# A leaky ReLU cut into two instructions, and a new order for the head of a kernel

## The chip, the cores and the metric

The kernel runs on one core of a Trainium2 chip. The metric is the device time of one launch in microseconds (us), as the median of several runs. Work inside the core is split over engines with a queue of their own each: TensorE (PE) multiplies matrices, VectorE (DVE) and GpSimd (POOL) do elementwise work, ScalarE (ACT) does activations and copies, SyncE (SP) starts transfers. An instruction starts when it is first in its engine's queue and the semaphores that it waits for have been raised.

## The reference

```python
def _attn_ref(x):                      # x: (8, 3008, 256)
    X = np.fft.fft(x, axis=1)
    X = np.fft.fft(X, axis=2)
    return X.real.astype(np.float32)

def _moe_ref(x, w_in, w_out):          # x: (24064, 256), w_in: (256, 2048), w_out: (2048, 256)
    h = x @ w_in
    g = np.maximum(0.01 * h, h)        # leaky ReLU
    return (g @ w_out).astype(np.float32)
```

The real part of a two-dimensional Fourier transform of each of 8 batches is taken, its rows go through a projection up to 2048 columns, a leaky ReLU, and a projection down to 256.

## The kernel before

The feature transform is folded into the weights: `fold_w_in` multiplies `w_in` by the cosine and sine tables, and gives `wf`. Of the transform along the sequence, a cosine part (`mixc`) and a sine part (`mixs`) are formed, and each hidden block is the sum of the two products for one column and the difference for the mirrored column. So a sum and a difference of two PSUM banks stand ahead of each leaky ReLU.

The work is laid out as chunks of columns. Most chunks go down with a scheme of sums and products that saves matmuls (class `Chunk`, lines 1173 to 1269 of the profile's rows). The first two pieces of 251 columns, `PLAIN = 2`, go straight through, since at the start the weights are still being loaded and converted: they are the **plain steps**. There are 16 of them, one for each piece `j` and pair `f` of hidden blocks; step n has f = n // 2 and j = n % 2 up to the last two, which are swapped. A plain step has these parts:

- `R:n` (`raised`, L951): eight PE rows in the trace, four into each of two PSUM banks of the ring `cos_psa, sin_psa, cos_psb, sin_psb`.
- `A:n` (`activate`): the cosine product gets its Nyquist term, either on DVE (L964, twice) or, for the steps of `SEEDED` and what follows them, by seeds that ACT writes into the bank ahead of the matmuls (L943, twice) and a copy (L960). Then DVE forms the sum (L971) and the difference (L972), 128x502 each, and ACT applies the leaky ReLU (L974) to both.
- `D0:n` and `D1:n` (`down_plain`, L996): four matmuls each (eight rows in the trace) that add the step's share to the lower or upper half of the output columns. Piece 0 adds into `sum_psa` and `sum_psb`, piece 1 into `sum_psc` and `dft_ps`. In each half the matmuls of the sum (r = 0) come ahead of those of the difference (r = 1).

Between the steps stands the work on the weights. `L:` starts a load on SP. `C:` converts one loaded block on DVE (L633, L642, L643 finish it, L625 and L626 begin the next, ACT's L627 and L628 stand between). `S:k` forms the sum and the difference of the two halves of a block of `w_in` (L675), on the engines of `HALVES_ON`: both on DVE for k = 1, both on POOL for k = 2, one on each for k = 3. `F:k` is the fold (L690): one PE group for the sum, one for the difference, and copies on ACT (L694). `T` loads four tables, `N` and `NF` load and fold the Nyquist column (POOL), `W:` forms sums of `w_out` on POOL (L718).

The order of all this is written out by hand: the text `HEAD` lists it, each word being issued to its engines in turn, and the dictionary `START` goes on with it beside the first steps of the first ordinary chunk. An instruction keeps its place in its own engine's queue, so two words that use different engines can change places without any effect.

```python
for op in HEAD.split():
    do(op)
rest()
```

In `START` the activations of steps 12 to 15 are not issued at once but handed on (`later`), and one ACT instruction (L1445) does them.

Of the kernel before, what the change touches and what calls it, by code (L numbers as in the profile page):

```python
# [12 lines left out]
ALU = mybir.AluOpType  # L13
ACT = mybir.ActivationFunctionType

B, S, D, F = 8, 3008, 256, 2048
# [25 lines left out]
NF = F // P  # L42
# [8 lines left out]
    0: "C:o6 D0:10 R:12 A:12",  # L51
    1: "D1:10 M:o7",
    2: "R:13 A:13",
    3: "D0:11 E:o7 W:2 W:3",
    4: "R:14 A:14 D1:11",
    5: "D0:12",
    6: "R:15 A:15",
    7: "D1:12",
# [2 lines left out]
    10: "D0:14",  # L61
    12: "D1:14",
    15: "D0:15",
    17: "D1:15",
}
ORDER = "w0a w0b o0 o1 w1a w1b o2 o3 w2a w2b o4 o5 w3a w3b o6 o7"
LOADED_EARLY = "o1 w1a w1b o2"
HEAD = """
L:o3 D0:0 R:1 B:o1 D1:0 A:2 R:3 C:o1 A:1 A:3 L:w2a C:w1a D0:2 D0:1 C:w1b D1:2 L:w2b D1:1 S:1 D0:3 F:1 D1:3 C:o2 R:4 L:o4 L:o5 A:4 C:o3 R:5 A:5 D0:4 C:w2a T D1:4 R:6 A:6 L:w3a D0:5 R:7 D1:5 C:w2b A:7 L:w3b L:o6 S:2 D0:6 F:2 C:o4 N D1:6 R:8 A:8 D1:7 C:o5 R:9 A:9 D0:7 NF D0:8 R:10 D0:9 C:w3a L:o7 A:10 C:w3b R:11 S:3 A:11 D1:8 F:3 D1:9 W:1 W:0
"""  # L70
EARLY = 14
FIRST_DOWN = 18.1
# [244 lines left out]
def tile_fnet_leaky_relu(  # L317
# [15 lines left out]
    nc = tc.nc  # L333
# [26 lines left out]
    def ring(tag):  # L360
        r = rings[tag]
        r[0] += 1
        return r[1][(r[0] - 1) % len(r[1])]
# [564 lines left out]
    def hidden_blocks(j, f):  # L928

        return 2 * f, 2 * f + 1  # L930

    def up(j, f):
        raised(j, f)
        activate(j, f)
# [3 lines left out]
    def seed_plain(j, f):  # L938

        b, c, at, n, _ = blocks[j]  # L940
        pt = seeded[j, f] = [up_ps(), up_ps()]
        for h, fh in enumerate(hidden_blocks(j, f)):
            nc.scalar.activation(pt[0][:, h * n : (h + 1) * n], nb_sb[:, at : at + n], ACT.Copy, scale=wn[:, fh : fh + 1])  # L943
# [11 lines left out]
    def activate(j, f, later=None):  # L955
        b, c, at, n, _ = blocks[j]
        fs, pt = hidden_blocks(j, f), raw.pop((j, f))
        cos = ring("cos")
        if (j, f) in seeded:
            nc.scalar.copy(cos[:, 0 : 2 * n], pt[0][:, 0 : 2 * n])  # L960
        else:
            for h in range(2):
                hs = slice(h * n, (h + 1) * n)
                nc.vector.scalar_tensor_tensor(cos[:, hs], in0=nb_sb[:, at : at + n],  # L964
                                               scalar=wn[:, fs[h] : fs[h] + 1],
                                               in1=pt[0][:, hs], op0=ALU.mult, op1=ALU.add)
        step = steps.index((j, f)) + 1
        if step in SEEDED:
            seed_plain(*steps[step])
        g = ring("g")[:, 0 : 4 * n].rearrange("p (r k) -> p r k", r=2)  # L970
        nc.vector.tensor_tensor(g[:, 0], cos[:, 0 : 2 * n], pt[1][:, 0 : 2 * n], op=ALU.add)  # L971
        nc.vector.tensor_tensor(g[:, 1], cos[:, 0 : 2 * n], pt[1][:, 0 : 2 * n], op=ALU.subtract)  # L972
        if later is None:
            nc.scalar.activation(g, g, ACT.Lrelu)  # L974
        else:
            later.append([g])
        a = [[g[:, r, h * n : (h + 1) * n] for h in range(2)] for r in range(2)]
        hidden[j, f] = a
# [506 lines left out]
    def do(op, later=None):  # L1485
# [17 lines left out]
        elif kind in ("R", "A", "D0", "D1"):  # L1503
            step = steps[int(at)]
            if kind == "R":
                raised(*step)
            elif kind == "A":
                activate(*step, later=later)
            else:
                down_plain(*step, halves=(int(kind[1]),))  # L1510
        elif kind == "S":
            sums_of[at] = sums_of_w_in([loaded[f"w{at}{a}"] for a in "ab"], [getattr(nc, e) for e in HALVES_ON[int(at) - 1]])
        elif kind == "F":
            fold_w_in(int(at) * WN, WN, [loaded.get(f"w{at}{a}") for a in "ab"], sums=sums_of.get(at))
        elif kind == "T":
            even_tables[:] = [[ring("s") for _ in range(2)] for _ in range(2)]
            for part in range(2):
                for i, first in enumerate((0, DW[0][0])):
                    nc.sync.dma_start(even_tables[part][i][:, 0 : DW[0][i]], direct_even[part, :, first : first + DW[0][i]])
        elif kind == "N":  # L1520
            nc.sync.dma_start(nyx, x_nyq)
        elif kind == "NF":
            fold_nyquist(0)
            rows = Rows(nya[:, 0], [nyz], 0, 0)
            rows.fold_even(nc.gpsimd)
            rows.fold_odd(nc.gpsimd)
            nyq_of.append(rows)
        else:
            assert kind == "W", op
            sum_weights(int(at))  # L1530
# [7 lines left out]
    with tc.manual_schedule(engines={mybir.EngineType.DVE, mybir.EngineType.PE, mybir.EngineType.SP}):  # L1538
        with tc.manual_schedule(engines={mybir.EngineType.Pool, mybir.EngineType.Activation}):
# [87 lines left out]
            store_nyquist(1, nyq_t)  # L1627
            spread_rest()
            activate(*steps[0])
            o.mantissa()  # L1630
            o.end()
# [45 lines left out]
```

## Time and profile before

| | us |
|---|---|
| median of 4 runs | 1822.67 (1822.64 to 1822.72) |
| the profiled execution | 1822.71 |
| its span, first to last instruction | 1820.9 |
| PE busy | 1811.0 (99%) |
| DVE busy | 1544.8 (85%) |
| ACT busy | 1135.6 (62%) |
| POOL busy | 1085.3 (60%) |

The profile comes from one execution. A row of a timeline has its start, how long it lasts (for merged rows, all of them together), the engine, the source line, the operation with its tiles, and in brackets how long the engine had been idle and which instruction released it. A matmul in float32 is two rows in the trace. Successive matmuls overlap, so the distance between two starts, and not a row's length, is what a group costs PE.

### The profile page before, as it was taken

The page shows a single profiled execution, that of the slowest core. Times are in us where ns is not written, and L with a number is a line of the kernel's source. Part 1 is how long each engine was busy: PE and PEld are TensorE (multiplying, and loading weights), DVE is VectorE, ACT ScalarE, POOL GpSimd, SP SyncE. Part 2 cuts the span into 40 slices and gives each one's busy share as a digit, 9 for nine tenths or more (in the row PEclk, how much of TensorE's full clock was granted, in tenths as well). Part 3 has the DMA queues.
Part 4 walks back from the last instruction along what each step waited for, and adds up shares of the span by engine and source line. Part 5 has one row for each costly group of instructions (what it writes and reads, how often), then busy time and mean ns, then how long its engine had stood idle before and what let it go on. Part 6 is the DMA issues. An engine that isn't in the chain of part 4 may idle for free.

```text
span 1820.9 us, 27070 instructions
## 1 busy us (share of the span) xinstructions
PE 1811.0 (99%) x9408; PEld 1540.0 (85%) x9408; DVE 1544.8 (85%) x3216; ACT 1135.6 (62%) x2319; POOL 1085.3 (60%) x590
## 2 busy tenths in 40 slices
PE   9999999999999999999999999999999999999999
PEld 7788888888888888888888888888888888888888
DVE  8869998897888978899787988879888798787678
ACT  4768666675666756566565666657666576565551
POOL 0156666565666665666665666656666666666660
PEclk9999999999999999999999999999999999999999
DMA  7312121202102011021101112010121110010000
GB/s 249 107 48 89 30 69 35 72 14 71 31 28 72 21 65 31 29 70 35 58 24 32 67 35 73 18 68 24 32 73 35 52 30 29 24 35 13 10 18 31
DMA packets 65897, 88.61 MB, mean 49 GB/s; under 512 B 10064, under 2 KB 53456, under 8 KB 65760
## 3 DMA queue, kind: packets, MB, share of 16 engines
q1 hardware_dynamic: 65616, 86.88, 14.5%
q8 instruction: 74, 1.21, 0.3%
q14 instruction: 63, 0.52, 0.1%
q10 hardware_dynamic: 144, 0.00, 0.0%
HBM read 62.12 MB, written 24.72 MB: 48 GB/s over the span
## 4 chain that ended last, share of the span: by engine, by line
PE 94%; DVE 4%; issue 1%; ACT 1%; POOL 0%; DMA 0%; DVEq 0%; POOLq 0%; ACTq 0%
PE sum_psc L1224 21%; PE sum_psa L1224 17%; PE sum_psb L1224 17%; PE cos_psa L1173 9%; PE sin_psa L1173 9%; PE cos_psb L1173 8%; PE sin_psb L1173 8%; PE dft_ps L756 3%; PE dft_ps L996 1%; DVE block L1203 1%; PE sum_psc L996 0%; PE sum_psb L996 0%; PE sum_psa L996 0%; DVE part L1269 0%; DVE block L971 0%
## 5 line engine op out<-in xcount | busy, mean ns | idle before, releaser
L1203 POOL TENSOR_TENSOR block<-block 128x752 f32<-128x752 f32 (+2 forms) x540 | 1045.4, 1948 | 609.0 <-DVE xt L1017 176.2
L1445 ACT ACTIVATE block<-block 128x376 f32<-128x376 f32 (+5 forms) x718 | 426.5, 623 | 4.3 <-DVE block L1186 3.6
L1203 DVE TENSOR_TENSOR block<-block 128x752 f32<-128x752 f32 (+2 forms) x328 | 416.6, 1274 | 0.2
L1186 DVE TENSOR_TENSOR block<-cos,sin_psa 128x376 f32<-128x376 f32 (+2 forms) x510 | 251.0, 533 | 140.8 <-PE sin_psa L1173 136.6
L1224 PEld LDWEIGHTS sum_psc<-block,wt 128*128 128x128 f32 x1736 | 289.3, 190 | 45.8 <-issue 0.5
L1224 PE MATMUL sum_psc<-block,wt 128*128 128x188 f32 (+2 forms) x1736 | 327.3, 321 | 0.4 <-DVE part L1269 0.4
L1186 DVE TENSOR_TENSOR block<-cos,sin_psb 128x376 f32<-128x376 f32 (+2 forms) x482 | 240.1, 539 | 102.8 <-PE sin_psb L1173 101.6
L1224 PE MATMUL sum_psa<-block,wt 128*128 128x188 f32 (+2 forms) x1736 | 312.2, 321 | 0.0
L1224 PEld LDWEIGHTS sum_psa<-block,wt 128*128 128x128 f32 x1736 | 283.5, 190 | 22.8
L1179 ACT COPY cos<-cos_psa 128x376 f32<-128x376 f32 (+2 forms) x255 | 119.0, 467 | 248.3 <-PE cos_psa L1173 245.6
L1179 ACT COPY cos<-cos_psb 128x376 f32<-128x376 f32 (+2 forms) x241 | 113.6, 472 | 210.8 <-PE cos_psb L1173 210.7
L1173 PE MATMUL cos_psa<-mixc,wf 128*128 128x376 f32 (+2 forms) x510 | 199.8, 473 | 0.5 <-ACT cos_psa L1168 0.5
L1173 PE MATMUL sin_psa<-mixs,wf 128*128 128x376 f32 (+2 forms) x510 | 199.8, 473 | 0.0
L1173 PE MATMUL sin_psb<-mixs,wf 128*128 128x376 f32 (+2 forms) x482 | 191.5, 479 | 0.0
L1173 PE MATMUL cos_psb<-mixc,wf 128*128 128x376 f32 (+2 forms) x482 | 191.4, 478 | 0.0
L1269 DVE TENSOR_TENSOR part<-part 128x188 f32<-128x188 f32 (+2 forms) x462 | 187.9, 444 | 1.9
L1224 PE MATMUL sum_psb<-block,wo 128*128 128x188 f32 (+2 forms) x992 | 188.0, 321 | 0.0
L1224 PEld LDWEIGHTS sum_psb<-block,wo 128*128 128x128 f32 x992 | 165.3, 190 | 22.8
L1224 PEld LDWEIGHTS sum_psb<-block,wt 128*128 128x128 f32 x992 | 163.5, 190 | 22.8
L1224 PE MATMUL sum_psb<-block,wt 128*128 128x188 f32 (+2 forms) x992 | 177.0, 321 | 0.0
L1168 ACT ACTIVATE cos_psa<-nb,wn 128x376 f32<-128x376 f32 (+2 forms) x255 | 145.9, 572 | 8.2
L1173 PEld LDWEIGHTS sin_psa<-mixs,wf 128*128 128x128 f32 x510 | 96.6, 189 | 61.7 <-DVE block L1186 0.4
(214 smaller groups left out, 1957.5 us busy)
## 6 DMA issues: line engine op xcount, KB each, us to landing
xt<-in_x_dram SPq DMA_DIRECT2D x28, 1024.0 KB, 5.4
out_dram<-part SPq DMA_DIRECT2D x176, 94.0 KB, 1.7
out_dram<-part SPq DMA_DIRECT2D x64, 94.5 KB, 1.7
tabe<-in_seq_tab_dram SPq DMA_DIRECT2D x29, 190.0 KB, 2.6
nb<-nyq_dram SPq DMA_DIRECT2D x23, 188.0 KB, 3.9
block<-in_w_in_dram SPq DMA_DIRECT2D x8, 512.0 KB, 5.6
block<-in_w_out_dram SPq DMA_DIRECT2D x8, 512.0 KB, 4.1
xt<-in_first_x_dram SPq DMA_DIRECT2D x4, 768.0 KB, 8.3
```

Source lines behind the costliest of these rows:

```text
L756: nc.tensor.matmul(o, lhsT=still, rhs=moving, start=(i == 0), stop=(i == 3), skip_group_check=True)
L996: nc.tensor.matmul(sums[j][d][:, r * n : (r + 1) * n], lhsT=wo[:, fs[h] // 4, fs[h] % 4, d], rhs=a[r][h], start=(f == 0 and r == 0 and h = ...
L1168: nc.scalar.activation(cos_ps[self.half(f)][:, 0 : self.w], columns_of(nb_sb, self.u, self.j, self.w), ACT.Copy, scale=wn[:, f : f + 1])
L1173: nc.tensor.matmul(bank[:, 0 : self.w], lhsT=wf[:, i, f * P : (f + 1) * P], rhs=columns_of(mix_sb[i], self.u, self.j, self.w), start=(i == ...
L1179: nc.scalar.copy(copy, cos[:, 0 : self.w])
L1186: nc.vector.tensor_tensor(block.row(to, g, self.n), x, y, op=op)
L1203: ins = (engine or nc.gpsimd).tensor_tensor(self.value(16 + i), xa, ya, op=ALU.add if sign > 0 else ALU.subtract)
L1224: nc.tensor.matmul(to, lhsT=weight(w)[:, g], rhs=self.value(v)[:, g], start=(first and at == 0), stop=(last and g == 3), skip_group_check= ...
L1269: ins = nc.vector.tensor_tensor(part_of[self.copy[v]][:, 0:n], xa, ya, op=ALU.add if sign > 0 else ALU.subtract)
L1445: nc.scalar.activation(to, to, ACT.Lrelu)
```

## The change

Two things are changed. In `activate`, a plain step's leaky ReLU becomes two instructions, one after the sum and one after the difference, each 128x502, where it was one of 128x1004; for the steps of `START` it stays as it is. And the lists `HEAD` and `START` get another order: `D1:2` goes ahead of `D0:1`, `D1:5` ahead of `D0:5` and `R:7`, `D0:8` behind `R:10`, `D1:9` ahead of `D1:8` and `F:3`, `D1:11` and `D1:15` one step earlier, beside words that move past words of other engines.

```diff
@@ START
-    3: "D0:11 E:o7 W:2 W:3",
-    4: "R:14 A:14 D1:11",
+    3: "D0:11 E:o7 D1:11 W:2 W:3",
+    4: "R:14 A:14",
...
-    17: "D1:15",
+    16: "D1:15",
+    17: "",
@@ HEAD
-L:o3 D0:0 R:1 B:o1 D1:0 A:2 R:3 C:o1 A:1 A:3 L:w2a C:w1a D0:2 D0:1 C:w1b D1:2 L:w2b D1:1 S:1 D0:3 F:1 D1:3 C:o2 R:4 L:o4 L:o5 A:4 C:o3 R:5 A:5 D0:4 C:w2a T D1:4 R:6 A:6 L:w3a D0:5 R:7 D1:5 C:w2b A:7 L:w3b L:o6 S:2 D0:6 F:2 C:o4 N D1:6 R:8 A:8 D1:7 C:o5 R:9 A:9 D0:7 NF D0:8 R:10 D0:9 C:w3a L:o7 A:10 C:w3b R:11 S:3 A:11 D1:8 F:3 D1:9 W:1 W:0
+L:o3 D0:0 R:1 B:o1 D1:0 A:2 R:3 C:o1 A:1 A:3 D0:2 L:w2a C:w1a C:w1b D1:2 D0:1 L:w2b S:1 D1:1 D0:3 F:1 D1:3 R:4 C:o2 L:o4 L:o5 A:4 C:o3 R:5 A:5 D0:4 C:w2a D1:4 R:6 L:w3a A:6 D1:5 T C:w2b D0:5 R:7 D0:6 A:7 S:2 L:w3b L:o6 F:2 C:o4 D1:6 R:8 A:8 N D1:7 R:9 C:o5 D0:7 A:9 R:10 NF C:w3a D0:8 A:10 L:o7 D0:9 C:w3b R:11 S:3 D1:9 W:1 D1:8 W:0 A:11 F:3
@@ activate
-        nc.vector.tensor_tensor(g[:, 0], cos[:, 0 : 2 * n], pt[1][:, 0 : 2 * n], op=ALU.add)
-        nc.vector.tensor_tensor(g[:, 1], cos[:, 0 : 2 * n], pt[1][:, 0 : 2 * n], op=ALU.subtract)
-        if later is None:
-            nc.scalar.activation(g, g, ACT.Lrelu)
-        else:
+        for r, op in enumerate((ALU.add, ALU.subtract)):
+            nc.vector.tensor_tensor(g[:, r], cos[:, 0 : 2 * n], pt[1][:, 0 : 2 * n], op=op)
+            if later is None:
+                nc.scalar.activation(g[:, r], g[:, r], ACT.Lrelu)
+        if later is not None:
             later.append([g])
```

## The prediction

> **What bounds the kernel now.** I read the page, then the busy times by stretch, then TensorE's own timeline between 30 and 92 us, because the change touches only the head of the program and the head is the only long stretch with holes in TensorE.
>
> ```profile
> PE 1811.0 (99%) x9408; PEld 1540.0 (85%) x9408; DVE 1544.8 (85%) x3216; ACT 1135.6 (62%) x2319; POOL 1085.3 (60%) x590
> ```
>
> TensorE (PE) is busy 1811.0 of 1820.9 us. No matmul is added or removed, so the time can move only by PE's waiting: 9.9 us in all. The windows say where the head's share lies and who is full beside it.
>
> ```profile
> 20.00:40.00 20.00, 18.90 (x92) 15.92 (x91) 19.16 (x44) 8.15 (x12) 0.00 (x0) 1.00 0.64 208
> 40.00:60.00 20.00, 19.41 (x86) 15.55 (x85) 17.49 (x33) 14.57 (x22) 0.00 (x0) 1.00 0.53 181
> 60.00:80.00 20.00, 19.29 (x87) 15.98 (x86) 16.18 (x30) 14.51 (x25) 5.95 (x10) 1.00 0.20 62
> 80.00:100.00 20.00, 19.04 (x84) 15.27 (x83) 16.52 (x30) 13.34 (x25) 11.30 (x10) 1.00 0.10 27
> ```
>
> Columns: PE, weight loads, DVE, ACT, POOL, granted clock (1.00 throughout, so no clock effect is expected). DVE is busy 19.16 of 20 us in the first of these: there it sets the pace, and PE's holes are its shadow. PE's timeline names each hole (in brackets the idle time and its releaser):
>
> ```profile
> 38.93 1.97 PE L996 MATMUL sum_psc<-block,wo 128*128 128x251 f32 x8 [0.57 <-ACT block L974]
> ...
> 45.88 1.13 PE L690 MATMUL sin_psa<-part,block 128*128 128x512 f32 x2
> ...
> 51.72 1.12 PE L951 MATMUL sin_psa<-mixc,wf 128*128 128x251 f32 x4 [0.41 <-ACT sin_psa L943]
> ...
> 53.87 1.97 PE L996 MATMUL sum_psa<-block,wo 128*128 128x251 f32 x8 [0.19 <-ACT block L974]
> ...
> 61.64 1.11 PE L951 MATMUL sin_psa<-mixc,wf 128*128 128x251 f32 x4 [0.71 <-ACT sin_psa L943]
> ...
> 66.85 1.02 PE L690 MATMUL sin_psb<-part,block 128*128 128x512 f32 x2
> 67.70 1.02 PE L690 MATMUL cos_psa<-block 128*128 128x512 f32 x2
> ...
> 82.70 1.11 PE L951 MATMUL sin_psb<-mixc,wf 128*128 128x251 f32 x4 [0.33 <-ACT sin_psb L943]
> ...
> 86.77 1.12 PE L690 MATMUL sin_psa<-part,block 128*128 128x512 f32 x2 [0.41 <-DVE part L675]
> 88.11 1.12 PE L690 MATMUL cos_psb<-block 128*128 128x512 f32 x2 [0.22 <-POOL block L675]
> ```
>
> The pipelined ends hide part of each hole, so I count **start delays**: unstalled, one half-step D takes 1.70 us from start to start (40.74 to 42.44), one R 1.70 (its two rows 0.85 each), one F 0.97 + 0.85 (45.88, 46.85, 47.70). Delays: 38.93 is 0.73 late (36.50 + 1.70 = 38.20), 45.88 0.04, 51.72 0.56, 53.87 0.34, 61.64 0.87 (59.07 + 1.70), 82.70 0.49, 86.77 0.57, 88.11 0.37 (86.77 + 0.97). Sum 3.97 us: the most that this change can reach. The delay at 29.64 (DVE's conversion L643) is ahead of everything moved and stays.
>
> **What the instruction queues become.** Built and compared, DVE and POOL keep their order; ACT keeps it too, but for twelve Lrelus made two each and two output copies moved up at 139.7; SP moves one weight load ahead of four table loads. So what the new table does is reorder PE: in the head one pair of D halves is swapped and three D halves pass R or F groups; two more move later.
>
> **The split.** Rows:
>
> ```profile
> L974 ACT ACTIVATE block<-block 128x1004 f32<-128x1004 f32 x12 | 12.5, 1042 | 14.2 <-DVE block L972 14.2
> ...
> L1445 ACT ACTIVATE block<-block 128x500 f32<-128x500 f32 x16 | 9.8, 610 | 0.0
> ```
>
> Half a Lrelu takes 0.61 by the 500-wide row. Today it starts when the difference (L972) ends and lasts 1.04. After, the first half starts when the sum (L971) ends, 0.59 earlier, and the second when the difference ends, done 1.04 - 0.61 = 0.43 earlier. ACT issues the next instruction about 0.09 before an end (79.55 after 78.60 + 1.04), so a pair costs 2 x 0.52 instead of 0.95: about 0.09 us more of ACT, twelve times 1.1 us, hidden because ACT works 14.6 of 20 us here at most and the pair still ends earlier.
>
> **Walk along PE, hole by hole** (lead = how much earlier than today).
>
> ```profile
> 45.14 0.69 DVE L675 TENSOR_TENSOR part<-block 128x512 f32<-128x512 f32 x1
> ```
>
> - 38.93: D1:2 now stands ahead of D0:1, so D0:1 comes 1.70 later and its Lrelu is there. Lead 0.73.
> - 45.88 (F:1) needs DVE's sum L675, done at 45.14 + 0.69 = 45.83. DVE's queue is the same and full, so that time stays. PE arrives near 45.1 and waits. **Lead back to 0.**
> - 51.72 (R:5) waits for the seeds L943 (50.71 + 0.96); ACT's queue ahead of them follows F:1. Stays.
> - 53.87 (D0:4): first half ready at 52.8, second at 53.38; PE wants them at 53.53 and 54.4. Lead 0.34; the seeds of R:6 (56.03 + 0.99 = 57.02) cut it to 0.3.
> - 61.64 (R:7): D1:5 now fills the 0.87 in front of it. Lead 1.17.
> - 66.85 (F:2): PE arrives at 65.7, but needs the two POOL sums:
>
> ```profile
> 64.76 1.27 POOL L675 TENSOR_TENSOR part<-block 128x512 f32<-128x512 f32 x1 [47.26 <-DVE block L643]
> ...
> 66.11 1.27 POOL L675 TENSOR_TENSOR block<-block 128x512 f32<-128x512 f32 x1
> 66.48 1.45 DVE L633 SCALAR_TENSOR_TENSOR wo<-block,wo 128x512 f32<-128x512 uint32 x1
> ```
>
> The second ends at 67.38. POOL follows DVE's L643, whose chain starts behind ACT's L960 and hardly moves (0.1 at most). So the second pair starts at 67.35 to 67.45 instead of 67.70. **Lead cut to about 0.35.**
> - 82.70 (R:11): PE would come at 82.21 - 0.35 = 81.86. The seeds (81.68 + 0.96 = 82.64) stand behind step 9's Lrelu on ACT, with small copies and L627, L628 between: they gain the 0.35 and the 0.43 of the split, and end near 81.86. Start about 81.9, lead 0.8.
> - 86.77 and 88.11 (F:3): D1:9 and D1:8 are now both ahead of it, one 1.70 more than today. PE arrives at about 87.05; the sums end at 86.02 + 0.69 and 86.79 + 1.27 = 88.06, each some 0.4 earlier behind the same lead, and the second is wanted at 88.0. Covered by 0.3; if that cover is gone it costs up to 0.94 again. Saved: 0.57 + 0.37, and 0.1 for a first matmul that no longer starts from a stop.
>
> Sum of the lead: 0.8 + 0.94 + 0.1 = **1.8 us**.
>
> **Edits taken at nothing.** The twelve doubled Lrelus (cover above). A:11 behind W in the list: DVE's and ACT's order is the same with it. The output copies of step 15 (139.74 and 140.19, 0.92 us of ACT) now precede a copy and the seed that starts at 138.19; the matmul that uses that seed starts at 140.67, and the seed would end near 139.7, so 1.0 us covers it; without cover 0.92. The four table loads (51.31 today) now stand behind a weight load that is issued at 54.65; with the 7.9 us that the slowest took to land they are there by 66, and PE uses them from 122.9. D1:11 directly behind D0:11 reads the same activations: no wait. Later holes (132.98: 0.54, 181.46: 0.36, 185.26: 0.52) follow the same queues and shift whole.
>
> **A rule of the skill.** The row first: L633 took 1.45 us at 66.48 beside POOL's sum, and 0.68 at 83.23 without one: 0.77 more. The Trainium skill, "SBUF — State Buffer", section "Who interferes with whom", says that a VectorE instruction with two SBUF inputs and a GpSimd instruction reading SBUF hold one port pair exclusively, the later fully blocked; L971 with a PSUM operand took 0.68 at 65.30 beside POOL, as it says. By that rule one collision could cost up to POOL's whole 1.27 instead of 0.77; it speaks against running PE ahead, since DVE's conversions then slide along POOL's work. The sum uses 0.77.
>
> **Rivals.**
> 1. *The gates take it all back.* F:2 and F:3 are set by DVE and POOL; if the POOL sums come no earlier and R:11's seeds keep their place, what is left is 0 to 0.9: 1821.8 to 1822.7. For it: F:1 does just that. Against: after 67.4 nothing but the seeds stands ahead of F:3. Chance 0.14.
> 2. *Every hole goes.* 3.97 us less: 1818.7. It needs DVE's sum at 45.14 to come earlier, and DVE has no idle time there. Chance 0.03.
> 3. *Slower: conversions collide with POOL ahead of F:3.* Eleven conversions with two SBUF operands (L633, L642, L643) lie on DVE between 68 and 86, ahead of F:3's sums. Each that newly runs beside a POOL instruction costs 0.77; F:3's cover takes 0.3. From three on (2.31 - 0.3 = 2.0) it outweighs the 1.8; with five, 1822.7 - 1.8 + 3.85 - 0.3 = 1824.4. For it: POOL has short work at 73 to 81 that is not tied to DVE. Against: those pieces last 0.2 to 0.76, and beside them L633 took 0.82 at 73.52 and L643 0.69 at 80.48. Chance 0.05.
>
> **How the numbers follow.** The profiled execution took 1822.71 us (span 1820.9 and 1.8 around it), the median 1822.67, so the sum carries over: 1822.7 - 1.8 = 1820.9. Chance 0.78; its own range is 1820.1 to 1821.7: 0.8 less if a hole of R:11's size (0.49) and a little of F:3's return, 0.8 more if the POOL sums of F:2 come earlier with the lead of 1.17. The range with half of rival 1 is 1819.9 to 1822.3; about 0.15 is left out. A 0.2% change is 3.6 us, about what a measurement of this kernel can tell from none: only rival 2 beats it downwards (0.02), and upwards it takes more than rival 3's five collisions (0.03).
>
> **What would show it.** Right: no PE idle at L974 and at F:3; a new wait of 0.6 or more at F:1 for DVE's L675 and at F:2 for POOL's; 51.72 unchanged; PE's row at 90.78 starting near 89.0. Wrong: F:1 starting well before 45.8, F:3 waiting still, or L633 rows of 1.4 us between 70 and 88.

## The result and the profile after

The changed kernel took **1820.97 us** (median of 34 runs, 1820.54 to 1821.83) where the kernel before took 1822.77 us beside it (52 runs, 1822.36 to 1823.38): ratio 0.999, 95% interval 0.9985 to 0.9995. That is 1.80 us less, 0.1%; by the interval it is between 0.9 and 2.7 us.

In the page after, TensorE (PE) is as busy as before and the span, 1819.2 instead of 1820.9 us, has lost only waiting:

```profile
PE 1810.9 (100%) x9408; PEld 1541.1 (85%) x9408; DVE 1544.9 (85%) x3216; ACT 1137.6 (63%) x2331; POOL 1085.2 (60%) x590
```

The busy times by stretch (length, PE, weight loads, DVE, ACT, POOL, granted clock, DMA share, GB/s) show that between 80 and 100 us PE now works without a hole, where it had worked 19.04 of 20 us:

```profile
60.00:80.00 20.00, 19.55 (x87) 16.00 (x86) 16.43 (x30) 15.93 (x31) 6.42 (x11) 1.00 0.32 107
80.00:100.00 20.00, 20.00 (x91) 16.76 (x90) 17.46 (x33) 14.41 (x25) 10.83 (x10) 1.00 0.11 28
```

PE's timeline after, for the places that the prediction walked along (its line numbers are one higher now: R is L952, F L691, S L676, D L997, seeds L944, the sum and difference L973, the leaky ReLU L975):

```profile
40.07 1.87 PE L997 MATMUL sum_psc<-block,wo 128*128 128x251 f32 x8
...
46.05 1.12 PE L691 MATMUL sin_psa<-part,block 128*128 128x512 f32 x2 [0.72 <-DVE part L676]
...
51.89 1.12 PE L952 MATMUL sin_psa<-mixc,wf 128*128 128x251 f32 x4 [0.41 <-ACT sin_psa L944]
...
53.69 1.86 PE L997 MATMUL sum_psa<-block,wo 128*128 128x251 f32 x8
...
66.22 1.13 PE L691 MATMUL sin_psb<-part,block 128*128 128x512 f32 x2 [0.23 <-POOL part L676]
67.58 1.13 PE L691 MATMUL cos_psa<-block 128*128 128x512 f32 x2 [0.23 <-POOL block L676]
...
82.13 1.03 PE L952 MATMUL sin_psb<-mixc,wf 128*128 128x251 f32 x4
...
87.25 1.02 PE L691 MATMUL sin_psa<-part,block 128*128 128x512 f32 x2
88.11 1.02 PE L691 MATMUL cos_psb<-block 128*128 128x512 f32 x2
88.97 1.86 PE L997 MATMUL sum_psa<-block,wo 128*128 128x251 f32 x8
90.69 1.11 PE L952 MATMUL cos_psb<-mixc,wf 128*128 128x251 f32 x4
```

D0:1 (here 40.07) and D0:4 (53.69) wait no more for a leaky ReLU, nor does R:11 (82.13) for its seeds or F:3 (87.25, 88.11) for its sums. In exchange F:1 waits 0.72 us for DVE and F:2 twice 0.23 us for POOL, which they did not before; R:5 (51.89) waits as it did. The last row is R:12, which before, with its two D (89.08 and 90.78) between it and F:3, was

```profile
92.48 1.01 PE L951 MATMUL cos_psb<-mixc,wf 128*128 128x251 f32 x4
```

One thing must be taken out when profiles are compared: the first D that DVE's conversion gates, ahead of every word that was moved, started at 29.64 us before and at 29.80 after, and anywhere from 29.43 to 29.80 in the profiles below. The edits do not sort these starts: where step 0's leaky ReLU is whole they run from 29.48 to 29.70, where it is two instructions from 29.43 to 29.80. So this table counts from that start. The last two columns should agree: R:12's start against that of before, and the medians' difference from before on the same chip.

| kernel | F:1 | R:6 | F:2, second pair | R:11 | F:3 | R:12 | R:12 earlier by | median less by |
|---|---|---|---|---|---|---|---|---|
| before | 16.24 | 27.74 | 38.06 | 53.06 | 57.13 | 62.84 | | |
| after | 16.25 | 27.43 | 37.78 | 52.33 | 57.45 | 60.89 | 1.95 | 1.80 |
| split alone | 16.25 | 27.43 | 38.04 | 52.62 | 57.16 | 62.87 | -0.03 | -0.04 |
| order alone | 16.26 | 27.75 | 37.80 | 52.73 | 57.93 | 61.35 | 1.49 | 1.40 |
| split 7, 9, 11 | 16.27 | 27.77 | 37.82 | 52.37 | 57.53 | 61.00 | 1.84 | 1.83 |
| split 9, 11 | 16.25 | 27.74 | 37.78 | 52.37 | 57.57 | 61.01 | 1.83 | 1.81 |
| split 9 | 16.24 | 27.73 | 37.78 | 52.33 | 57.48 | 61.34 | 1.50 | 1.44 |
| D1:9 behind F:3 | 16.25 | 27.43 | 37.78 | 52.33 | 56.74 | 62.46 | 0.38 | 0.37 |
| DVE's sum twice | 16.97 | 28.15 | 38.50 | 53.05 | 58.15 | 61.57 | 1.27 | 0.94 |
| R:5's seeds early | 16.24 | 27.42 | 37.76 | 52.31 | 57.41 | 60.83 | 2.01 | 1.95 |
| F:2's sums shared | 16.26 | 27.46 | 37.12 | 52.04 | 57.24 | 60.67 | 2.17 | 2.28 |
| shared and seeds | 16.25 | 27.43 | 37.08 | 52.05 | 57.26 | 60.67 | 2.17 | 2.23 |

R:12 has the same matmuls ahead of it in every row, and the holes behind it keep their size (the one at 132.98 before is at 131.28 after, 0.54 both times). The 95% intervals of the ratios below are about 0.0009 to either side, 1.6 us: wider than most of the differences. The medians follow R:12's start to within 0.15 us in all rows but one, so the readings rest on the trace and the medians stand beside it. Each trace is of one execution; how well they repeat shows in F:1, which starts at 16.24 to 16.27 in all eleven rows where nothing was added ahead of it.

### The profile page after: what moved, and what is told of

It reads as the page before. It is cut to its first block, busy times and chain, and to the rows that moved or that the text cites. A ratio compares the mean times of both kernels' runs of the same rounds, so it can differ in the third digit from the quotient of the medians.

```text
span 1819.2 us, 27087 instructions
## 1 busy us (share of the span) xinstructions
PE 1810.9 (100%) x9408; PEld 1541.1 (85%) x9408; DVE 1544.9 (85%) x3216; ACT 1137.6 (63%) x2331; POOL 1085.2 (60%) x590
## 3 DMA queue, kind: packets, MB, share of 16 engines
q8 instruction: 74, 1.21, 0.3%
## 4 chain that ended last, share of the span: by engine, by line
PE 96%; DVE 3%; issue 0%; POOL 0%; ACT 0%; DVEq 0%; POOLq 0%
PE sum_psc L1225 21%; PE sum_psa L1225 17%; PE sum_psb L1225 17%; PE cos_psa L1174 9%; PE sin_psa L1174 9%; PE sin_psb L1174 8%; PE cos_psb L1174 8%; PE dft_ps L757 3%; PE sum_psa L1537 1%; PE dft_ps L997 1%; DVE block L1204 1%; DVE block L973 0%; PE sum_psb L997 0%; PE sum_psc L997 0%; PE sum_psa L997 0%
```

## The experiments

All start from the changed kernel unless said otherwise.

**1. The split alone.** The tables of before, the two instructions of after.

```diff
-HEAD, START of the changed kernel
+HEAD, START of the kernel before
```

> The leaky ReLU in two instructions, with HEAD and START of before. Theory (gates): the delays of 38.93 (0.73) and 53.87 (0.34) go, but the first lead is taken back by F:1, which waits for DVE's sum at 45.9 (new idle of about 0.7 there), the second by R:7, whose seeds stand behind L628 and no Lrelu. R:11 comes about 0.4 earlier, and F:3 takes that back too, because its sums stay at 86.7 and 88.0. Left: 0 to 0.3 us faster than before. Rival (the split pays by itself): 0.73 + 0.34 + 0.43 = 1.5 us faster, with F:1, R:7 and F:3 earlier by as much.

Measured: 1822.78 us against 1822.74, ratio 1.0 (0.9991 to 1.0009). PE's timeline of this run:

```profile
61.68 1.11 PE L951 MATMUL sin_psa<-mixc,wf 128*128 128x251 f32 x4 [0.89 <-ACT sin_psa L943]
...
82.32 1.12 PE L951 MATMUL sin_psb<-mixc,wf 128*128 128x251 f32 x4
86.86 1.12 PE L690 MATMUL sin_psa<-part,block 128*128 128x512 f32 x2 [0.86 <-DVE part L675]
```

The split does what it says: D0:1 no longer waits, D0:4 and R:6 come 0.3 us earlier, and R:11 0.44 us (52.62 where it was 53.06). Then F:1 waits 0.72 us for DVE, which it did not before, R:7 waits 0.89 instead of 0.71 us and F:3 0.86 instead of 0.41. All three are set by other engines, and nothing is left. D0:1's wait goes here without D1:2 ahead of it, and F:1 comes no later, so that move adds nothing to the split.

**2. The order alone.** The new tables, one leaky ReLU of 128x1004.

```diff
-        for r, op in enumerate((ALU.add, ALU.subtract)):
-            ...
+        nc.vector.tensor_tensor(g[:, 0], ..., op=ALU.add)
+        nc.vector.tensor_tensor(g[:, 1], ..., op=ALU.subtract)
+        if later is None:
+            nc.scalar.activation(g, g, ACT.Lrelu)
```

> The new HEAD and START, with the leaky ReLU in one instruction. Theory (the two parts need each other): up to F:2 as in the changed kernel (lead 0.35), but the ACT work behind a whole Lrelu comes 0.43 later: the copies of F:2 ahead of R:8, the seeds of R:11 (a delay of 0.4 to 0.8 at R:11), and the copies of F:3 ahead of R:12. F:3 itself stays covered. 0.6 to 1.2 us faster than before. Rival (the order does it all): 1.8 us faster, as the changed kernel.

Measured: 1821.34 against 1822.74 us, ratio 0.9992 (0.9984 to 1.0001): 1.40 us less, a little above the range expected, which had assumed waits of R:8 and R:12 for copies that did not come. PE's timeline shows R:11 still at its gate:

```profile
82.21 1.11 PE L952 MATMUL sin_psb<-mixc,wf 128*128 128x251 f32 x4 [0.21 <-ACT sin_psb L944]
```

It starts 0.40 us later than in the changed kernel, and R:12 0.46 later. R:12 itself has no wait here: it starts at 90.83, one D (1.70) behind 89.13. The parts do not add: 0.0 for the split and 1.4 for the order make 1.8 together (by R:12's start 0.0, 1.5 and 1.95).

**3. Three steps split.** `later is None and step - 1 in (7, 9, 11)` for the two instructions, one for the rest.

```diff
-            if later is None:
+            if later is None and step - 1 in (7, 9, 11):
                 nc.scalar.activation(g[:, r], g[:, r], ACT.Lrelu)
+        if later is None and step - 1 not in (7, 9, 11):
+            nc.scalar.activation(g, g, ACT.Lrelu)
```

> The changed kernel with only the steps 7, 9 and 11 (counted from 0) in two instructions, the other nine in one. Theory: halves pay only where ACT has copies or seeds for PE directly behind that Lrelu: step 7 ahead of the copies of F:2, step 9 ahead of the seeds of R:11, step 11 ahead of the copies of F:3. Step 4's 0.3 comes back at D0:4 (53.87) and is taken by F:2's POOL sums. So 1.8 us faster than before, the same as the changed kernel within 0.2. Rival (each split gives its share): three of twelve, so about a quarter of what lies between e2 and the changed kernel.

Measured: 1820.91 against 1822.74 us, ratio 0.999 (0.9981 to 0.9999): the changed kernel's time with three pairs instead of twelve. In PE's timeline D0:4 again waits for its whole leaky ReLU:

```profile
53.87 1.97 PE L999 MATMUL sum_psa<-block,wo 128*128 128x251 f32 x8 [0.18 <-ACT block L977]
```

R:6 is 0.34 us later for it, and F:2 takes that back (37.82, the changed kernel 37.78).

**4. F:2's sums shared.** S:2's sum goes to DVE, its difference stays on POOL, and S:2 is put ahead of step 7's activation.

```diff
-HALVES_ON = (('vector', 'vector'), ('gpsimd', 'gpsimd'), ('vector', 'gpsimd'))
+HALVES_ON = (('vector', 'vector'), ('vector', 'gpsimd'), ('vector', 'gpsimd'))
-... D0:6 A:7 S:2 L:w3b ...
+... D0:6 S:2 A:7 L:w3b ...
```

> The changed kernel with S:2's sum on DVE and its difference on POOL (HALVES_ON of k = 2), and S:2 listed ahead of A:7. Theory (F:2 is gated by the POOL sums, 66.22 and 67.58 with two waits): DVE stands idle 0.68 at 64.75, where the sum (0.69) fits, and POOL's difference follows it, done near 66.8: the second pair of F:2 starts near 66.9, 0.6 to 0.7 earlier. ACT's copies of F:2 stand behind step 7's Lrelu and give R:8 a new wait of up to 0.3. So 2.0 to 2.3 us faster than before, 0.3 to 0.5 faster than the changed kernel. Rival (the later seeds of R:11 take it all): no faster than the changed kernel.

Measured: 1820.46 against 1822.74 us, ratio 0.9988 (0.9979 to 0.9996): 2.28 us less, the lowest median of all. PE's timeline and POOL's and DVE's beside it:

```profile
65.50 1.02 PE L691 MATMUL sin_psb<-part,block 128*128 128x512 f32 x2
66.57 1.12 PE L691 MATMUL cos_psa<-block 128*128 128x512 f32 x2
```
```profile
65.24 1.28 POOL L676 TENSOR_TENSOR block<-block 128x512 f32<-128x512 f32 x1 [47.93 <-DVE part L676]
```
```profile
64.47 0.69 DVE L676 TENSOR_TENSOR part<-block 128x512 f32<-128x512 f32 x1
...
66.30 0.77 DVE L634 SCALAR_TENSOR_TENSOR wo<-block,wo 128x512 f32<-128x512 uint32 x1
```

F:2's second pair starts 0.66 us earlier than in the changed kernel; by R:12 0.22 remains, by the medians 0.48. So F:2's POOL sums were a gate. Of the 0.66 us, R:8 (0.15 late, at 69.38) and R:11 (0.13 late, at 81.49) take back a part. The sign is the same in trace and medians; how much of the half microsecond is real is below what the times can tell.

**5. D1:9 back behind F:3.**

```diff
-S:3 D1:9 W:1 D1:8 W:0 A:11 F:3
+S:3 D1:8 W:1 W:0 A:11 F:3 D1:9
```

> The changed kernel with D1:9 behind F:3 again (D1:8 and A:11 ahead of it, as before). Theory (F:3's sums set its start, the extra D covers the wait): F:3 is reached 1.70 earlier and waits about 0.9 for DVE's sum and 0.4 for POOL's: the 0.94 and the 0.1 come back, so about 0.8 us faster than before instead of 1.8. The copies of F:3 ahead of R:12 get D1:9 as cover again. Rival (F:3 was late because PE was late; with the lead it waits no more): 1.8 us, as the changed kernel.

Measured: 1822.41 against 1822.78 us, ratio 0.9998 (0.9989 to 1.0006): 0.37 us less than before, so this one move is worth 1.43 of the 1.80 (by R:12's start 1.57 of 1.95). The other moves, D1:2, D1:5 and D0:8, were not taken back one by one. PE's timeline at F:3:

```profile
86.17 1.12 PE L691 MATMUL sin_psa<-part,block 128*128 128x512 f32 x2 [0.84 <-DVE part L676]
87.53 1.13 PE L691 MATMUL cos_psb<-block 128*128 128x512 f32 x2 [0.23 <-POOL block L676]
```

R:11 is where the changed kernel has it (52.33), but PE then comes to F:3 a D early and waits for both sums.

**6. DVE's sum twice.** The sum for F:1 is issued a second time, so DVE has 0.72 us more ahead of F:1.

```diff
+        if made[0] is loaded["w1a"]:
+            nc.vector.tensor_tensor(sums[0], a, b, op=ALU.add)
```

> The changed kernel with S:1's sum (128x512, 0.69 on DVE) issued twice, the same values again. Theory (DVE's full queue sets F:1, and everything after follows F:1): F:1 starts 0.70 to 0.75 later, R:5, F:2, R:11 and the end too, since their waits hang on DVE and ACT work that follows F:1. So 1.0 to 1.1 us faster than before instead of 1.8, a price of 0.7. Rival (a later gate has slack and absorbs it, F:2's POOL sums for one): no more than 0.3 of it reaches the end.

Measured: 1821.84 against 1822.78 us, ratio 0.9995 (0.9986 to 1.0004): 0.86 us of the gain lost. PE's timeline at F:1:

```profile
46.47 1.12 PE L693 MATMUL sin_psa<-part,block 128*128 128x512 f32 x2 [1.44 <-DVE part L678]
```

PE's wait at F:1 doubles from 0.72 to 1.44, and everything from F:1 to R:12 comes 0.68 to 0.72 us later. As far as R:12, DVE's queue ahead of F:1 goes into the time nearly one to one: no lead that PE wins ahead of F:1 can count.

**7. R:5's seeds early.** They are issued right behind R:4, ahead of the conversions that stood before them on ACT.

```diff
-F:1 D1:3 R:4 C:o2 L:o4
+F:1 D1:3 R:4 s:5 C:o2 L:o4
...
+        elif kind == "s":
+            seed_plain(*steps[int(at)])
```

> The changed kernel with the seeds of R:5 (L944, twice) listed right behind R:4, ahead of C:o2 and its ACT work. Theory (F:2's POOL sums take back any lead that DVE does not share): R:5 no longer waits at 51.9 (0.56 earlier), but F:2 still starts where POOL lets it; the lead turns into longer waits at R:6 or F:2. 1.6 to 2.0 us faster than before, the same as the changed kernel. Rival (a removed hole is a gain): 0.5 faster than the changed kernel, 2.3 faster than before.

Measured: 1820.83 against 1822.78 us, ratio 0.999 (0.9981 to 0.9998). In PE's timeline R:5's hole is gone, and a new one stands one step on:

```profile
51.30 1.01 PE L952 MATMUL sin_psa<-mixc,wf 128*128 128x251 f32 x4
...
57.21 1.11 PE L952 MATMUL sin_psb<-mixc,wf 128*128 128x251 f32 x4 [0.54 <-ACT sin_psb L944]
```

R:6's seeds gate it: R:6 starts at 27.42, as in the changed kernel (27.43), and all behind it is within 0.06 us.

**8. Only step 9 split.** As experiment 3, with `step - 1 == 9`.

> The changed kernel with only step 9 (counted from 0) in two instructions. Theory (two ACT chains, one behind the other: the seeds of R:11 behind step 9's Lrelu, the copies of F:3 behind step 11's): R:11 starts 0.4 earlier than with no split, but R:12 then waits as much for the copies of F:3, which stand behind step 11's whole Lrelu. 1.3 to 1.5 us faster than before, the same as with the order alone (1.4). Rival (step 9 alone carries what the split gives): 1.8 us faster, as the changed kernel.

Measured: 1821.34 against 1822.78 us, ratio 0.9992 (0.9983 to 1.0001): the time of the order alone, although R:11 starts where the changed kernel has it. PE's and ACT's timelines show what holds R:12:

```profile
81.93 1.06 PE L952 MATMUL sin_psb<-mixc,wf 128*128 128x251 f32 x4
90.94 1.11 PE L952 MATMUL cos_psb<-mixc,wf 128*128 128x251 f32 x4 [0.28 <-ACT wf L695]
```
```profile
87.56 1.04 ACT L977 ACTIVATE block<-block 128x1004 f32<-128x1004 f32 x1 [1.35 <-DVE block L973]
...
89.71 1.17 ACT L695 COPY wf<-cos_psb 64x512 f32<-64x512 f32 x2
```

Step 11's leaky ReLU ends at 88.60, F:3's four copies stand behind it on ACT, the last ends at 90.88, and R:12, which multiplies by what they write, starts at 90.94. In the changed kernel the same part of ACT's queue reads

```profile
87.15 1.21 ACT L975 ACTIVATE block<-block 128x502 f32<-128x502 f32 x2 [0.77 <-DVE block L973]
88.38 1.18 ACT L695 COPY wf<-sin_psa 64x512 f32<-64x512 f32 x2
89.47 1.17 ACT L695 COPY wf<-cos_psb 64x512 f32<-64x512 f32 x2
```

There the pair ends at 88.36, the copies at 90.64, and R:12 starts at 90.69, 0.05 later: it is at its gate there too.

**9. Steps 9 and 11 split.** As experiment 3, with `step - 1 in (9, 11)`.

> The new order, and only steps 9 and 11 apply their leaky ReLU in two instructions. Theory (two chains on ACT are all that the split is worth: step 9's to the seeds of R:11, and step 11's to the copies of F:3 that R:12 waits for): same as the changed kernel, about 1.8 us below before, 1820.9 to 1821.0; R:11 starts about 52.3 us after the first D that DVE's conversion gates, R:12 about 60.9. Rival (step 7 or another step carries part of it): between the order alone and the changed kernel, 1821.1 to 1821.3, with R:11 or R:12 0.2 to 0.4 us later than that.

Measured: 1821.05 against 1822.86 us, ratio 0.9991 (0.9982 to 0.9999): 1.81 us less, the changed kernel's gain. R:11 at 52.37 and R:12 at 61.01, expected 52.3 and 60.9. Two pairs are enough. Step 11 split alone was not run; by experiment 2, where R:12 has no wait, nothing is there for it to save.

**10. Shared sums and early seeds together.** Experiments 4 and 7 in one kernel.

> The sums for F:2 shared by DVE and POOL, and the seeds of R:5 ahead of the conversions, together. By themselves the first gave 0.5 us beyond the changed kernel and the second nothing, since F:2's sums on POOL took it back. Gates theory: with the sums shared F:2's second half still starts 0.1 us after it could (66.57 where 65.50 + 0.97 = 66.47), and R:8 and R:11 wait a little, so of the 0.56 us of R:5's removed delay at most 0.2 remains: 1820.2 to 1820.5. Rival (the gate at F:2 is gone, so the removed hole now counts in full): 0.5 us less, about 1819.9, and F:2 starts 0.5 us earlier in relation to the first D that DVE's conversion gates (35.5 instead of 36.05).

Measured: 1820.63 against 1822.86 us, ratio 0.9989 (0.998 to 0.9998): 2.23 us less, as with the shared sums alone (2.28), and 0.1 us above the range expected. F:2 starts at 36.03 (36.05 there), so the rival's 35.5 is out. But the theory named the wrong gate. It expected F:2 to take the hole back; PE's timeline shows that R:6's seeds have done so before F:2 is reached:

```profile
56.95 1.11 PE L952 MATMUL sin_psb<-mixc,wf 128*128 128x251 f32 x4 [0.54 <-ACT sin_psb L944]
```

## Why the prediction was right, and where its steps were not

**The sum.** 1.8 us were forecast and 1.80 measured. The mechanism, leads that gates take back, is shown by experiment 1 (F:1, R:7 and F:3), 3 (F:2), 6 (F:1) and 7 (R:6): what is saved ahead of such a start while another engine sets it is worth nothing.

In the trace R:12 leads by 1.95, and the sum of the walk was 0.8 + 0.94 + 0.1 = 1.84. R:11 leads by 0.73 instead of 0.8. Between R:11 and R:12 1.22 is gained instead of 1.04, and the term that was too small is the 0.1 for a first matmul that starts from a stop: before, three groups there did so, R:11 itself (0.95 to its second row, 0.87 after) and both pairs of F:3 (the second 0.97 to the next start, 0.86 after), so it is about 0.3. That the medians give 1.80 exactly is chance, within an interval of 0.9 to 2.7.

**F:1.** A new wait of at least 0.6 us for DVE and no lead: 0.72, start 16.25 against 16.24. **R:5** unchanged: 0.41 again. **R:6**: lead cut to 0.3: 0.31, and experiments 7 and 10 show the seeds as its gate. **F:2**: PE could have come at 62.44 + 1.70 + 1.70 = 65.84, 36.04 from the first D, 1.17 ahead of before as the walk said; its second pair leads by 0.28 instead of 0.35, and the waits are POOL's, for both pairs: idle twice 0.23, or 0.38 and 0.39 as start delays, 0.77 together where a wait of 0.6 or more was the sign. POOL's second sum starts 36.45 us from the first D, before 36.47, so it hardly moved, as forecast. **R:11**: a lead of 0.8 forecast, 0.73 found, and no wait. **F:3**: no wait. POOL's sum for the second pair ends at 86.61 + 1.28 = 87.89, 0.22 ahead of its start, where 0.3 of cover was forecast. **The D at 90.78** starts at 88.97, forecast near 89.0. **Step 15's output copies**, taken at nothing: the seed behind them ends at 138.26 and its matmul starts at 138.94 without a wait, 0.68 of cover where 1.0 was forecast.

**Rival 1**, all taken back, was right that F:1 and F:2 take back what is won ahead of them (R:6, which it does not name, does so too) and wrong behind them. **Rival 2**, every hole goes, is refuted by F:1, which did not come earlier in any run. **Rival 3**, collisions on DVE, did not come about: ahead of F:3 the only long conversion is the one at F:2's sums that was there before. DVE's timeline after:

```profile
66.61 1.46 DVE L634 SCALAR_TENSOR_TENSOR wo<-block,wo 128x512 f32<-128x512 uint32 x1
```

Those at 73.43, 78.25 and 83.05 take 0.80, 0.69 and 0.69.

**What the walk got wrong.** It stopped at F:3. Moving D1:9 ahead of F:3 also takes it from between F:3 and R:12, where it had covered F:3's copies: before, two D stood there, 3.4 us; after, one. R:12 then starts 0.05 us behind the end of the copies, and it does so that early only because step 11's leaky ReLU is two instructions. The prediction saw a gain in two of the twelve splits, step 9's 0.43 and step 4's share at D0:4. Step 9's was right in size (0.44 at R:11 in experiment 1, 0.40 in experiment 2). Step 4's is worth nothing (experiments 3 and 9). Step 11's was missed: without it 0.33 us are lost at R:12 and 0.37 by the medians (experiments 8 and 9). Steps 9 and 11 work in series: with the order alone R:11's gate puts R:12 at 61.35, with step 9 split as well the copies put it at 61.34, and only with both does it come to 61.01. The forecast came out right all the same, since R:12's gate happened to fall where PE arrived (88.97 + 1.70 = 90.67, start 90.69). That is luck: the walk had no term for this gate, neither for the cover taken away nor for the split that made up for it.

**D1:9's price.** The expectation of experiment 5 put it at 1.0 us, from the prediction's 0.57 + 0.37 + 0.1; it is 1.43. In experiment 5 R:11 starts at 81.76, so F:3 could start one R and one D later, at 85.16, and its second pair 0.97 after 86.17. They start 1.01 and 0.39 late, 1.40 together: PE reaches this place earlier than before, and DVE's sum does not follow all the way. The 0.57 had been counted behind a later R:11.

**Breaking up an instruction.** The Trainium skill, "Perfetto Trace Analysis", section "Optimizing Scalar/DVE Operations", says that where ScalarE or VectorE is not saturated but causes bubbles on other engines, "breaking up instructions may allow work to be completed sooner". The runs agree for two of twelve instructions, and put a condition beside it: the engine that waited must not meet another engine's gate before the time is used. With the old order all twelve together gave 0.0 us.

## What to carry to other kernels

List the starts that another engine's queue sets, and add up leads only from the last of them on; beyond the slack that such a gate had, a lead ahead of it is worth nothing, and a hole removed there comes back at the next gate. When a group is moved ahead of a wait to fill it, look also at the wait that it covered where it stood. Two gates in series hide each other: here step 9's split alone showed nothing, and with step 11's it brought 0.3 us. So test such fixes together before one is dropped.

## What the runs showed of the hardware

The price of a collision between DVE and POOL was taken as a fixed 0.77 us. It is not fixed. After, the conversion L634 began at 66.61, while POOL's sum ran from 66.25 to 67.53, and ended at 68.07, 0.54 after POOL. In experiment 4 it began at 66.30, with only 0.22 of POOL's sum left, lasted 0.77 and ended at 67.07, 0.55 after POOL. Before, it ended at 66.48 + 1.45 = 67.93, 0.55 after POOL's 67.38. So in all three it ends 0.55 us after POOL's instruction, as if it had been held until then: the price is what POOL has left to do, less about 0.15. The conversion that begins beside F:3's POOL sum says the same (after, 87.62 + 0.81 = 88.43, 0.54 after POOL's 87.89), and all twelve profiles give 0.54 or 0.55 at both places. That fits the exclusive lock that the Trainium skill describes in "SBUF — State Buffer", section "Who interferes with whom". None of these began early enough in a POOL instruction of 1.27 us to pay all of it. The dearest lies behind R:12: before, the one at 95.74 took 1.70 beside POOL's sum L718 (95.62 to 96.90), 1.02 more than the 0.68 of one alone, and ended 0.54 after it. That is more than the prediction's 0.77 and less than its bound of 1.27; its sum needed neither, since no new collision came ahead of F:3.

The twelve pairs raised ACT's busy time by 2.0 us (1135.6 to 1137.6), 0.17 each, as 1.21 for a pair against 1.04 for the whole says. The prediction's 0.09 is what a pair takes longer in ACT's queue, where instructions overlap by about that much. It could not be read apart here, since the second half mostly waits for the difference.
